# Where the first block's down product keeps its first operand sums, and when the next block's transposing transfers are issued

## The chip, the cores and the metric

The kernel runs on one core of one Trainium2 chip. The metric is device time in microseconds (us) for one execution. A core has five engines that work beside each other and meet at semaphores: TensorE (PE, matrix products), VectorE (DVE), ScalarE (ACT), GpSimd (POOL) and SyncE (SP). SP, ACT and POOL also issue DMA transfers, each from its own queue and in its own order. An engine executes its instructions in the order in which the program lists them, so an instruction that waits holds up everything behind it on that engine.

## The reference, cut to what matters

```python
def reference(A_x, A_wqkv, A_wo, B_x, B_w1, B_w3, B_w2):
    x = A_x                                   # 1 x 2048 x 1024, bf16
    xn = layernorm(x)
    # attention: 32 heads of 32, each position sees 8 positions, 2 apart
    q, k, v = split(xn @ wqkv)                # 1024 x 3072
    o = softmax(q . k[pos - 2*w] * scale) @ v[pos - 2*w]     # w = 0..7
    s = o @ wo                                # 1024 x 1024
    # gated MLP on the same xn
    h = silu(xn @ w1) * (xn @ w3)             # 1024 x 3584 each
    g = silu(h @ w2)                          # 3584 x 1024
    return x + s * g
```

`B_x` is not used. The change touches `h @ w2`, the down product, and the way in which the layer-normed `x` of the next rows reaches the tile from which the next products read it.

## The kernel before, in words

**Rows.** The 2048 rows are worked in two blocks (b = 0, 1) of 1024 rows. A block is two chunks of 512 rows (c = 2b and 2b + 1), a chunk is four steps of 128 rows (`st`, or `g` in the down product). The tile `xT` holds the normed x of the block, transposed: half 0 for the even chunk, half 1 for the odd chunk, in each half 8 row tiles of 512 columns.

**Products.** The large products are written with seven part products instead of eight (2 x 2 blocks, with sums and differences of blocks formed ahead on DVE). For the up products the sums of x stand in the tile `xs` (four parts, fp16). For the down product the blocks are two rows of h (`row` 0 and 1, one for each chunk), two halves of the 3584 inner columns (`fh`) and two halves of the 1024 output columns. The four sums of h are called s1 to s4; s2, s3 and s4 overwrite h in place, s1 has a place of its own. The sums of w2 (called t) were formed in the first block and written to `t_dram`.

**The down product `mlp_down`** of block 0 has seven products in this order. I number them P1 to P7: P1 and P2 (h row 0 with w2), P3 (s2 with T2), P4 (s1 with T1), P5 (s3 with w2), P6 (s4 with T3) and P7 (h row 1 with T4). Each is 4 steps g of 14 matmuls (128 x 128 times 128 x 512), and each streams two operand loads of 896 KB, first and second half. The sums s1, s3 and s2 are written on DVE between P1 and P3. After P4 of a step g, ACT copies the bank (`dsp`), and only then may P5 add to the same bank.

**Buffers for loads.** The operand loads, the x rows of the next chunks, and the weights of what follows share six buffers named `r8`. `Plan.place` (L68) gives each new tile, in the order in which the code lists the work, the buffer whose last user comes earliest in that list. In block 0's down product this gives, with letters for the six buffers:

| tile | first half | second half |
|---|---|---|
| P1 | A | B |
| x of chunk 2, x of chunk 3 | C | D |
| P2 | E | F |
| P3 | A | B |
| P4 | E | F |
| P5 | A | B |
| P6 | E | F |
| P7 | A | B |
| `wo` (two loads), behind P7 | C | E |

**The next block's x.** While block 0's down product runs, the x rows of chunks 2 and 3 are loaded, and ACT takes each chunk's mean and variance (`ln_act`, L430 and L433), the root (L436), and normalises the four steps (L443). DVE adds two tiny instructions for each chunk (L439, L440). Then `ln_td` (L469) issues one transposing transfer for each step from ACT's queue: eight in all, into `xT`. The code lists them with P6 (chunk 2) and P7 (chunk 3).

**Where s1 stands.** `s1v` (L909) puts s1 of steps 0 and 1 into half 0 of `xT` and of steps 2 and 3 into half 1: in each half all but the last of the eight row tiles, 128 of each 256 columns for each step. The cells that follow reads and writes (`s1_cells`, L367) make a transposing transfer wait until P4 has read the s1 that lies under it.

**Order.** Nothing is issued in the order of the code. `Plan` builds the dependences, gives each instruction a due time, and then runs a list schedule: an engine that becomes free takes, of the instructions that are ready, the one with the earliest due time. PE keeps the order of the code. The due time of any other instruction is the earliest due time of those that need it, less its own duration (`limits`, L127). A transfer that fills a buffer is one of those that need the buffer's last users. The durations are constants in the code: 1.3 us of ACT for a transposing transfer, among others. The schedule is made when the program is built; on the chip each engine keeps the order that came out.

Of the kernel before, what the change touches and what calls it, by code (L numbers as in the profile page):

```python
# [224 lines left out]
def kernel(  # L225
# [12 lines left out]
    P = 128  # L238
    S, D, F = 2048, 1024, 3584
    Dh, W, DIL = 32, 8, 2  # L240
    KT = D // P
# [3 lines left out]
    NB = S // BL  # L245
    NST = CH // P
    FT = F // P
    FH = FT // 2
# [4 lines left out]
    NQ = 7  # L253
# [73 lines left out]
    def mm(ps, lhs, rhs, first, rd, last=True, mark=(), st=None):  # L327

        n = len(lhs)
        cut = (lambda a: a) if st is None else (lambda a: a[:, st * P:(st + 1) * P])  # L330

        def emit():
            for k in range(n):
                nc.tensor.matmul(  # L334
                    cut(ps.ap()), lhsT=lhs[k](), rhs=cut(rhs[k]()), start=(first and k == 0),
                    stop=(last and k == n - 1), skip_group_check=not (first and last) or st is not None,
                )
# [16 lines left out]
    def dma(eng, name, o, a, rd, wr, kb, run=1024, late=0.0):  # L354
        e = {SP: nc.sync, POOL: nc.gpsimd, ACT: nc.scalar}[eng]
        occ = {SP: 0.45, POOL: 0.58, ACT: 0.55}[eng]
        plan.op(eng, name, lambda: e.dma_start(out=o(), in_=a()), rd, wr, occ, 0.0, nbytes=kb * 1024, late=late, run=run)
# [5 lines left out]
    def xt_cells(half, kh, st=None):  # L363
        return [("xT", half, (kh * KH + k) * 2 + q // 2, q % 2) for k in range(KH)
                for q in (range(4) if st is None else [st])]

    def s1_cells(g):  # L367
        return [("xT", g // 2, f, g % 2) for f in range(FH)]

    def xs_cells(i):  # L370
        return [("xs", i, k) for k in range(KH)]
# [7 lines left out]
    def r8v(s, dt=BF16):  # L379
        a = s.ap()  # L380
        return a.bitcast(dt) if dt != BF16 else a
# [20 lines left out]
    def xrow(xt, st):  # L402
        return xt.ap().rearrange("p (s d) -> p s d", s=NST)[:, st, :]
# [65 lines left out]
    def ln_td(c, st, xt):  # L469

        half = c % 2
        plan.op(ACT, f"td{c}_{st}", lambda: nc.scalar.dma_start_transpose(  # L472
            out=xT[:, half, :, st * P:(st + 1) * P], in_=xrow(xt, st)),
            [(xt, st)], xt_cells(half, 0, st) + xt_cells(half, 1, st), 1.3, 0.0, nbytes=256 * 1024, run=256)
# [272 lines left out]
    def flush():  # L747
        while pend:
            pend.pop(0)()
# [131 lines left out]
    def mlp_down(b):  # L881
        G = range(NST)
        R = [range(0, FH), range(FH, FT)]
        F_ = [slice(0, FH), slice(FH, FT)]
        gs = [[slice(rr * CH + g * P, rr * CH + (g + 1) * P) for g in G] for rr in range(2)]
# [23 lines left out]
        s1v = lambda g: xT16[:, g // 2].rearrange("p k n -> p (k n)")[:, 0:FH * 256].rearrange(  # L909
            "p (f n) -> p f n", f=FH)[:, :, (g % 2) * P:(g % 2 + 1) * P]  # L910
# [4 lines left out]
        NS = FH * P  # L915
        rhs = rhs_load("w", 0, 0)
        xn = []
        for c in range(2 * b + 2, 2 * b + 4 if b + 1 < NB else 0):
            xt = plan.slot("r8", f"x{c}")
            xn.append(xt)  # L920
            for st in range(NST):
                x_load(c, st, xt)
            ln_act(c, range(NST), xt)
        pa, pb = [], []
        for g in G:
            if g == 2:
                flush()
            pa.append(bank(f"da{b}_{g}"))
            prod(pa[g], g, 0, 0, rhs, True, BF16)
        for g in G:  # L930
            tt("s1", add, lambda g=g: s1v(g), hb(0, 1, g), hb(1, 1, g), hcl(0, 1, g) + hcl(1, 1, g), s1_cells(g), NS, True)
            tt("s3", sub, hf(0, 1, g), hb(0, 0, g), hb(0, 1, g), hcl(0, 0, g) + hcl(0, 1, g), hcl(0, 1, g), NS, True)
        for g in G:
            pb.append(bank(f"db{b}_{g}"))
            cp("dfork", pb[g].ap, pa[g].ap, [pa[g]], [pb[g]])
            tt("s2", sub, hf(0, 0, g), lambda g=g: s1v(g), hb(0, 0, g), s1_cells(g) + hcl(0, 0, g), hcl(0, 0, g), NS, True)
        rhs = rhs_load("w", 1, 0)
        for g in G:
            prod(pa[g], g, 0, 1, rhs, False, BF16)
            gsilu(2 * b, 0, g, pa[g].ap, [pa[g]], 0.48)  # L940
        rhs = rhs_load("t", t=T2)
        su2 = []
        for g in G:
            tt("s4", sub, hf(1, 0, g), hb(1, 0, g), hf(0, 0, g), hcl(1, 0, g) + hcl(0, 0, g), hcl(1, 0, g), NS, True)
        for g in G:
            prod(pb[g], g, 0, 0, rhs, False, FP16)
            su2.append(plan.slot("k2", "dsu"))
            cp("dsu", lambda g=g: f32(su2[g]), pb[g].ap, [pb[g]], [su2[g]])
        rhs = rhs_load("t", t=T1)
        pe, sp5 = [], []  # L950
        for g in G:
            pe.append(bank(f"de{b}_{g}"))
            for q, (wt, ops) in enumerate(rhs):
                mm(pe[g], [lambda g=g, k=k: s1v(g)[:, k, :] for k in range(q * NQ, (q + 1) * NQ)], ops, q == 0,
                   [wt] + s1_cells(g), last=q == 1)
            sp5.append(plan.slot("k2", "dsp"))
            cp("dsp", lambda g=g: f32(sp5[g]), pe[g].ap, [pe[g]], [sp5[g]])
        rhs = rhs_load("w", 1, 1)
        for g in G:
            prod(pe[g], g, 0, 1, rhs, False, FP16)  # L960
            tt("dsb", add, lambda g=g: f32(su2[g]), pe[g].ap, lambda g=g: f32(su2[g]), [pe[g], su2[g]], [su2[g]], 512, False)
            gsilu(2 * b, 1, g, lambda g=g: f32(su2[g]), [su2[g]], 0.54)
        rhs = rhs_load("t", t=T3)
        for g in G:
            if b + 1 < NB:
                ln_td(2 * b + 2, g, xn[0])
            prod(pb[g], g, 1, 0, rhs, False, FP16)
            tt("dsa", add, lambda g=g: f32(sp5[g]), pb[g].ap, lambda g=g: f32(sp5[g]), [pb[g], sp5[g]], [sp5[g]], 512, False)
            gsilu(2 * b + 1, 1, g, lambda g=g: f32(sp5[g]), [sp5[g]], 0.54)
        rhs = rhs_load("t", t=T4)  # L970
        for g in G:
            if b + 1 < NB:
                ln_td(2 * b + 3, g, xn[1])
            prod(pb[g], g, 1, 1, rhs, False, BF16)
            gsilu(2 * b + 1, 0, g, pb[g].ap, [pb[g]], 0.48)

# [242 lines left out]
```

## Time and profile before

| what | value |
|---|---|
| median of the runs shown | 728.86 us (3 runs, 727.54 to 733.38) |
| the profiled execution's own time | 730.64 us |
| span of that execution, first to last instruction | 728.8 us |
| mean granted TensorE clock | 0.994 |
| VectorE busy | 640.3 us (88%) |
| ScalarE busy | 383.2 us (53%) |
| transposing transfers | 8, issued from 297.3 to 318.6 us, 8.8 us from issue to landing (median) |
| P2, P3, P4 begin (TensorE) | 269.81, 281.9, 293.98 us |
| P5 begins | 306.06 us |

Times in the profile count from the first instruction of the span. A row of the timeline gives start, duration, engine (a name with a q is the engine's queue: issuing a transfer, or waiting on a semaphore), the line of the code, the operation, and what it writes and reads; "x2" merges two neighbours, and the bracket at the end gives the idle time of the engine just before and what ended it. In the groups and waits, L334 is the line that emits the matmuls, L343 that of all two-operand DVE instructions, L348 that of ACT copies, L357 that of plain transfers, and L472 that of transposing transfers; so a row is told apart by its tiles. Starts that stand inside a merged row were read from narrower windows of the same timeline (P3's from P2's start and 56 matmuls).

### The profile page before, as it was taken

To read this page: it belongs to the slowest core of one execution; us is meant where nothing else is said; L and a number is where in the kernel's file an instruction comes from. 1 tells how busy PE (TensorE), PEld (TensorE's weight loads), DVE (VectorE), ACT (ScalarE), POOL (GpSimd) and SP (SyncE) were. 2 spreads that over 40 slices of the span, in tenths; PEclk is the share of its full clock that TensorE was granted. 3 is DMA by queue.
4 is the path that set the end of the run, shared out by engine and by line. 5 is a ranking of instruction groups with operands and counts; after the bars stand their busy time and mean duration, and the time that the engine had idled before them with its cause. 6 is when DMAs were issued, how large, how long until landed. Compare 5 with 4: busy or idle time off the path is not lost.

```text
span 728.8 us, 9155 instructions
## 1 busy us (share of the span) xinstructions
PE 714.8 (98%) x3372; PEld 345.6 (47%) x3372; DVE 640.3 (88%) x860; ACT 383.2 (53%) x656; POOL 25.5 (4%) x54
## 2 busy tenths in 40 slices
PE   7999999999999999998999999999999999999997
PEld 5655544444444444443455554444444444444443
DVE  6998999798999999359999899789999967999527
ACT  7754465575656698232444544675565656212233
POOL 0011000100000000000000000000000000000000
PEclk9999999999999999999999999999999999999999
DMA  9869865875546654997355449987555356463522
GB/s 333 303 239 395 278 245 170 274 218 211 179 172 210 224 165 139 208 275 224 115 174 173 169 149 318 295 291 223 188 175 190 115 214 208 152 193 112 173 73 101
DMA packets 127053, 150.54 MB, mean 207 GB/s; under 512 B 12320, under 2 KB 103968, under 8 KB 122656
## 3 DMA queue, kind: packets, MB, share of 16 engines
q1 hardware_dynamic: 113248, 121.65, 51.7%
q0 software_dynamic: 5312, 26.22, 9.5%
q10 hardware_dynamic: 8448, 2.10, 1.9%
q8 instruction: 26, 0.43, 0.3%
q14 instruction: 19, 0.16, 0.1%
HBM read 106.95 MB, written 32.51 MB: 191 GB/s over the span
## 4 chain that ended last, share of the span: by engine, by line
PE 87%; DVE 5%; DMA 4%; ACTq 2%; ACT 1%; issue 0%; SPq 0%; DVEq 0%
PE mm L334 87%; ACTq L472 2%; DVE r L343 2%; DMA r<-in_A_wqkv_dram 2%; DVE h_sb L343 1%; DMA r<-t_dram 1%; DVE xs L343 1%; DMA r<-in_A_x_dram 1%; DVE qo L343 1%; DMA r<-in_B_w_dram 0%; DVE small L411 0%; ACT k L348 0%; PE mm L456 0%; ACT xT L463 0%; DVE r L419 0%
## 5 line engine op out<-in xcount | busy, mean ns | idle before, releaser
L334 PEld LDWEIGHTS <-r 128*128 128x128 f16 (+1 forms) x2288 | 240.6, 107 | 244.5 <-issue 1.5
L334 PE MATMUL mm<-xs,r 128*128 128x512 f16 x1280 | 295.5, 379 | 0.7 <-DVE h_sb L343 0.7
L334 PE MATMUL mm<-xT,r 128*128 128x512 bf16 (+1 forms) x1008 | 228.2, 371 | 0.0
L348 ACT COPY k<-mm 128x512 f32<-128x512 f32 x192 | 111.9, 588 | 94.9 <-PE mm L334 80.2
L334 PE MATMUL mm<-r,h_sb 128*128 128x512 bf16 (+1 forms) x704 | 155.6, 382 | 4.2 <-DMA r<-t_dram 2.5
L343 DVE TENSOR_TENSOR att<-att 128x2048 bf16<-128x2048 bf16 (+4 forms) x132 | 123.7, 952 | 29.5 <-DMA att<-E 20.2
L334 PEld LDWEIGHTS <-h_sb 128*128 128x128 f16 (+1 forms) x800 | 78.7, 98 | 100.2 <-issue 7.1
L348 ACT COPY mm<-mm 128x512 f32<-128x512 f32 x88 | 49.8, 572 | 75.4 <-PE mm L334 49.1
L343 DVE TENSOR_TENSOR att<-qo,kT 128x2048 bf16<-128x2048 bf16 x64 | 77.2, 1216 | 1.6 <-ACT kT L348 1.6
L343 DVE TENSOR_TENSOR att<-E,vT 128x2048 bf16<-128x2048 bf16 x56 | 65.9, 1218 | 0.0
L351 ACT ACTIVATE k<-k 128x512 bf16<-128x512 f32 x56 | 34.8, 631 | 54.8 <-DVE k L343 54.8
L343 DVE TENSOR_TENSOR h_sb<-mm,k 128x512 bf16<-128x512 f32 x96 | 62.2, 682 | 0.4 <-PE mm L334 0.2
L343 DVE TENSOR_TENSOR k<-mm,k 128x512 f32<-128x512 f32 x72 | 47.8, 682 | 13.8 <-PE mm L334 13.7
L343 DVE TENSOR_TENSOR r<-r,r 128x1024 f16<-128x1024 bf16 (+4 forms) x66 | 52.1, 797 | 5.2 <-DMA r<-in_A_wqkv_dram 5.1
L343 DVE TENSOR_TENSOR h_sb<-h_sb,k 128x1024 bf16<-128x1024 bf16 x56 | 36.9, 685 | 12.0 <-ACT k L348 12.0
L351 ACT ACTIVATE h_sb<-mm 128x512 bf16<-128x512 f32 x60 | 35.6, 598 | 20.6 <-PE mm L334 20.3
L343 DVE TENSOR_TENSOR qo<-qo,att 128x2048 bf16<-128x2048 bf16 x32 | 38.9, 1217 | 0.0
L348 ACT CAST k<-mm 128x512 bf16<-128x512 f32 x56 | 32.6, 588 | 10.6 <-PE mm L334 10.3
L343 DVE TENSOR_TENSOR h_sb<-h_sb 128x512 f16<-128x512 bf16 (+1 forms) x72 | 36.6, 570 | 0.0
L343 DVE TENSOR_TENSOR r<-r 128x1024 f16<-128x1024 bf16 (+1 forms) x34 | 25.7, 777 | 0.0
L334 PE MATMUL mm<-r,xT 128*128 128x512 f16 x112 | 24.5, 379 | 0.0
L334 PE MATMUL mm<-h_sb 128*128 128x512 f16 x96 | 22.0, 379 | 0.0
(74 smaller groups left out, 336.9 us busy)
## 6 DMA issues: line engine op xcount, KB each, us to landing
r<-in_B_w_dram SPq DMA_DIRECT2D x42, 512.0 KB, 4.1
s_dram<-r POOLq DMA_DIRECT2D x14, 1024.0 KB, 5.4
r<-t_dram SPq DMA_DIRECT2D x16, 896.0 KB, 6.4
r<-s_dram SPq DMA_DIRECT2D x14, 1024.0 KB, 4.9
r<-in_A_wqkv_dram SPq DMA_DIRECT2D x12, 1024.0 KB, 6.9
r<-in_B_w_dram SPq DMA_DIRECT2D x12, 896.0 KB, 5.4
h_sb<-in_B_w_dram SPq DMA_DIRECT2D x14, 512.0 KB, 9.8
t_dram<-h_sb POOLq DMA_DIRECT2D x14, 512.0 KB, 5.9
```

The costliest lines, as they stand in the source:

```text
L334: nc.tensor.matmul(cut(ps.ap()), lhsT=lhs[k](), rhs=cut(rhs[k]()), start=(first and k == 0), stop=(last and k == n - 1), skip_group_check= ...
L343: plan.op(DVE, name, lambda: fn(out=o(), in0=a(), in1=b()), rd, wr, occ, 0.08, late=late)
L348: plan.op(ACT, name, lambda: nc.scalar.copy(out=o(), in_=a()), rd, wr, occ, 0.11)
L351: plan.op(ACT, name, lambda: nc.scalar.activation(out=o(), in_=a(), func=ACTF.Silu), rd, wr, occ, 0.11, table="silu")
L472: plan.op(ACT, f"td{c}_{st}", lambda: nc.scalar.dma_start_transpose(out=xT[:, half, :, st * P:(st + 1) * P], in_=xrow(xt, st)), [(xt, st)] ...
```

## The change: what it does

For block 0 alone (`b` is 0), s1 moves. Steps 0, 1 and 2 go to the first three of the four parts of `xs`, 14 x 128 columns each. Step 3 goes to half 1 of `xT`, columns 256 to 511 of its first seven row tiles; its sums and what reads them are written with one more dimension (`fold`). Block 1 keeps the old places; there are no transposing transfers in it.

The calls of `ln_td` move up in the code: those of chunk 2 from P6 to P2; those of chunk 3 from P7 to between P3's loads and P3 (steps 0 and 1) and to between P5's loads and P5 (steps 2 and 3).

```diff
-    def s1_cells(g):
-        return [("xT", g // 2, f, g % 2) for f in range(FH)]
+    def s1_cells(b, g):
+        if b:
+            return [("xT", g // 2, f, g % 2) for f in range(FH)]
+        return xs_cells(g) if g < 3 else [("xT", 1, 2 * k + 1, t) for k in range(KT) for t in range(2)]
...
+        fold = lambda a, g: a if b or g < 3 else a.rearrange("p (k h) n -> p k h n", h=2)
...
+        def s1v(g):
+            if b:
+                return xT16[:, g // 2].rearrange("p k n -> p (k n)")[:, 0:FH * 256].rearrange(
+                    "p (f n) -> p f n", f=FH)[:, :, (g % 2) * P:(g % 2 + 1) * P]
+            if g < 3:
+                return xs[:, g].rearrange("p k n -> p (k n)")[:, 0:NS].rearrange("p (f n) -> p f n", f=FH)
+            return xT16[:, 1, 0:NQ, 256:512].rearrange("p k (h n) -> p k h n", h=2)
+
+        def s1t(g, k):
+            return s1v(g)[:, k, :] if b or g < 3 else xT16[:, 1, k // 2, 256 + k % 2 * P:256 + (k % 2 + 1) * P]
...
         rhs = rhs_load("w", 1, 0)
         for g in G:
+            if xn:
+                ln_td(2 * b + 2, g, xn[0])
             prod(pa[g], g, 0, 1, rhs, False, BF16)
             gsilu(2 * b, 0, g, pa[g].ap, [pa[g]], 0.48)
         rhs = rhs_load("t", t=T2)
+        for st in (0, 1) if xn else ():
+            ln_td(2 * b + 3, st, xn[1])
...
         rhs = rhs_load("w", 1, 1)
+        for st in (2, 3) if xn else ():
+            ln_td(2 * b + 3, st, xn[1])
...
         rhs = rhs_load("t", t=T3)
         for g in G:
-            if b + 1 < NB:
-                ln_td(2 * b + 2, g, xn[0])
             prod(pb[g], g, 1, 0, rhs, False, FP16)
...
         rhs = rhs_load("t", t=T4)
         for g in G:
-            if b + 1 < NB:
-                ln_td(2 * b + 3, g, xn[1])
             prod(pb[g], g, 1, 1, rhs, False, BF16)
```

More of the change, by code (lines that the diff above doesn't have):

```diff
@@ L884, in mlp_down @@
         F_ = [slice(0, FH), slice(FH, FT)]
+        NS = FH * P
+        fold = lambda a, g: a if b or g < 3 else a.rearrange("p (k h) n -> p k h n", h=2)
         gs = [[slice(rr * CH + g * P, rr * CH + (g + 1) * P) for g in G] for rr in range(2)]
@@ L907, in prod @@
                    [wt] + h_cells(fs, row, [g]), last=q == 1)
-        s1v = lambda g: xT16[:, g // 2].rearrange("p k n -> p (k n)")[:, 0:FH * 256].rearrange(
-            "p (f n) -> p f n", f=FH)[:, :, (g % 2) * P:(g % 2 + 1) * P]
+        def s1v(g):
[7 more added lines that the diff above has]
+            return s1v(g)[:, k, :] if b or g < 3 else xT16[:, 1, k // 2, 256 + k % 2 * P:256 + (k % 2 + 1) * P]
         hb = lambda fh, row, g: (lambda: h_sb[:, F_[fh], gs[row][g]])
@@ L914, in mlp_down @@
         hcl = lambda fh, row, g: h_cells(R[fh], row, [g])
-        NS = FH * P
         rhs = rhs_load("w", 0, 0)
@@ L930, in mlp_down @@
         for g in G:
-            tt("s1", add, lambda g=g: s1v(g), hb(0, 1, g), hb(1, 1, g), hcl(0, 1, g) + hcl(1, 1, g), s1_cells(g), NS, True)
+            tt("s1", add, lambda g=g: s1v(g), lambda g=g: fold(hb(0, 1, g)(), g), lambda g=g: fold(hb(1, 1, g)(), g), hcl(0, 1, g) + hcl(1, 1, g), s1_cells(b, g), NS, True)
             tt("s3", sub, hf(0, 1, g), hb(0, 0, g), hb(0, 1, g), hcl(0, 0, g) + hcl(0, 1, g), hcl(0, 1, g), NS, True)
@@ L935, in mlp_down @@
             cp("dfork", pb[g].ap, pa[g].ap, [pa[g]], [pb[g]])
-            tt("s2", sub, hf(0, 0, g), lambda g=g: s1v(g), hb(0, 0, g), s1_cells(g) + hcl(0, 0, g), hcl(0, 0, g), NS, True)
+            tt("s2", sub, lambda g=g: fold(hf(0, 0, g)(), g), lambda g=g: s1v(g), lambda g=g: fold(hb(0, 0, g)(), g), s1_cells(b, g) + hcl(0, 0, g), hcl(0, 0, g), NS, True)
         rhs = rhs_load("w", 1, 0)
         for g in G:
+            if xn:
+                ln_td(2 * b + 2, g, xn[0])
             prod(pa[g], g, 0, 1, rhs, False, BF16)
@@ L953, in mlp_down @@
             for q, (wt, ops) in enumerate(rhs):
-                mm(pe[g], [lambda g=g, k=k: s1v(g)[:, k, :] for k in range(q * NQ, (q + 1) * NQ)], ops, q == 0,
-                   [wt] + s1_cells(g), last=q == 1)
+                mm(pe[g], [lambda g=g, k=k: s1t(g, k) for k in range(q * NQ, (q + 1) * NQ)], ops, q == 0,
+                   [wt] + s1_cells(b, g), last=q == 1)
             sp5.append(plan.slot("k2", "dsp"))
```

## The prediction, made before the changed kernel was run

> **What bounds the kernel.** I read the page's first part, then what TensorE waited for, then the timeline of block 0's down product.
>
> ```profile
> PE 714.8 (98%) x3372; PEld 345.6 (47%) x3372; DVE 640.3 (88%) x860; ACT 383.2 (53%) x656; POOL 25.5 (4%) x54
> ...
> PE mm L334 <- DMA r<-t_dram: 2.5, 1, 2.5
> ...
> PE mm L334 <- ACT k L348: 1.7, 1, 1.7
> ```
>
> TensorE is the bound: 14.0 us idle in 728.8, some 9.8 of it ahead of the first products and behind the last. Inside the run two waits stand out, 2.5 and 1.7 us, both in this down product. No change here can win more than these two and what hangs on them.
>
> ```profile
> 297.26 6.23 ACTq L472 DMA_TRANSPOSE xT<-r  x2
> 303.53 0.59 ACT L348 COPY k<-mm 128x512 f32<-128x512 f32 x1 [5.75 <-PE mm L334]
> 303.56 5.51 ACTq L472 DMA_TRANSPOSE xT<-r  x2
> ...
> 309.19 7.12 ACTq L472 DMA_TRANSPOSE xT<-r  x2
> ...
> 316.35 0.59 ACT L348 COPY k<-mm 128x512 f32<-128x512 f32 x1 [6.65 <-issue]
> 316.37 4.65 ACTq L472 DMA_TRANSPOSE xT<-r  x2
> 316.99 16.78 PE L334 MATMUL mm<-r,h_sb 128*128 128x512 bf16 x77 [1.69 <-ACT k L348]
> ...
> 327.78 1.22 SPq L357 DMA_DIRECT2D E<-att  x2
> ...
> 329.10 0.54 SPq L357 DMA_DIRECT2D r<-t_dram  x1
> ...
> 336.30 12.42 PE L334 MATMUL mm<-r,h_sb 128*128 128x512 f16 x49 [2.54 <-DMA r<-t_dram]
> ```
>
> This is the timeline from P4's end on. Eight transposing transfers hold ACT's queue for 23.5 us (6.23 + 5.51 + 7.12 + 4.65), and the `dsp` copies stand between them. The fourth copy, ready when P4 ends (306.2), runs at 316.35; P5's last step waits for it: the 1.69 us. The exponential of the next attention also stands behind the transfers (321.19, idle 4.25 before it), so its results leave for `E` only at 327.78. P7's second load stands behind these on SP's queue: its buffer is free when P5 ends (about 320), it is issued at 329.10, lands at 336.26, and TensorE waits 2.54 us.
>
> ```profile
> 327.00:333.00 6.00, 6.00 (x30) 2.70 (x29) 6.00 (x8) 1.56 (x4) 1.11 (x2) 1.00 0.65 176
> 333.00:339.00 6.00, 3.46 (x13) 1.34 (x12) 5.61 (x7) 2.14 (x4) 0.00 (x0) 0.86 1.08 359
> 339.00:345.00 6.00, 6.00 (x25) 2.57 (x24) 6.00 (x8) 0.74 (x2) 0.00 (x0) 0.86 0.40 146
> ```
>
> The windows (the figure behind POOL is the granted clock) show a price behind that second wait: the clock falls to 0.86 over 12 us, half of it slow. P7's last 49 matmuls go from 336.30 to 348.56, where the next product begins: 12.26 us against 49 x 0.2158 = 10.57 at the pace of P2 to P4 (56 in 12.085). That is 1.69 us more. The first wait left the clock at 1.00. So what can go is 1.69 + 2.54 + 1.69 = **5.92 us**. A rule speaks against the third term: the Trainium skill, "TensorE: Matmul & The Clock Gate", section "What's actually happening", has the clock drop after at least one idle window of about 3.4 us. By it a gap of 2.54 us would leave the clock alone and the sum would be 4.23 us; the row of 0.86 decides against it.
>
> **The change part by part.** *s1's new place.* The four sums keep their count; a sum takes 1.083 us. Matmuls with `xs` and with `xT` both take 379 ns: nothing there. The folded sums of step 3 are not in the trace: at half rate they would cost 2 x 1.08 us of DVE, at best nothing; I take nothing, since they keep the row's element counts. P3's step 3 needs the second of them at 291 us, DVE wrote it by 278.3. Either end is hidden by 12 us.
>
> *The transposing transfers no longer wait for P4* (but for the last two). Still eight, from the same queue. What lets them start is the normalising, now at 283.64 to 294.2, since nothing needed it early. So the move alone would gain about 2 us of start.
>
> *The buffers turn over differently*, and this decides. With chunk 2's last user listed in P2, buffer C is free for P4. By the rule of `place`: P3 keeps A, B; P4 gets **C** and E; P5 F, A; P6 B, C; P7 E and **D** (chunk 3's); `wo` F, A. So P4's first load must wait until all four transfers of chunk 2 have landed, and P7's second load for those of chunk 3. The due times follow: P4's load is due before P4, so chunk 2's transfers, normalising, root and variances get due times ahead of all of chunk 3's work and of P2's activations, where they had been the last of all.
>
> I place them by hand, with the trace's durations. Chunk 2's statistics start at 250.18 as now; a mean with its read-out takes 1.05 us, a variance 1.13, four pairs 8.7; eight copies and activations due earlier come between (about 4.0): 262.9. Root with its table load 1.6, two `uc` copies 1.0: 265.5. The two tiny DVE instructions each stand behind one of about 1.1: 266.6. Four normalisings 4 x 1.14, two `dfork` copies 1.0, and the rest of a started chunk 3 statistic: the transfers start at about **273**, before P4 by 21 us. The two `uc` copies come about 1.5 us later than now, and so does the first sum; P3 needs s2 at 281.9 and has it at 271.2 now: hidden by 9 us.
>
> How long do four transfers take? Contended, in the rows above, from the first issue (297.3) to the fourth landing, which released the load of `wo` into C (315.44): 18.1 us. Alone:
>
> ```profile
> q10 hardware_dynamic: 1719, 0.42, 100.4%
> ...
> 276.00:278.00 2.00, 2.00 (x11) 0.88 (x9) 2.00 (x3) 1.98 (x5) 0.00 (x0) 1.00 0.00 0
> 278.00:280.00 2.00, 2.00 (x11) 0.93 (x10) 2.00 (x3) 1.97 (x3) 0.00 (x0) 1.00 0.00 0
> ```
>
> The first row is the transposing queue from 308 to 310 us: 1719 packets in 2 us. A transfer is 1056 of them (8448 over eight), so 1.23 us. The windows show that now no DMA runs from 276 to 280. P3's loads end at 276; then four transfers take 4.9 us of DMA; with the tail of a landing I put the last at **284** (bounds 280 and 291.1, the latter by the contended 18.1). P4's first load then takes 6.3 us (median of the four T2 and T1 loads): **290.3**, bounds 286 and 297.4. P4 starts at 293.98. I take no wait, as that stretch lies nearer to the idle row than to the contended one. Of the rate, the Trainium skill, "Advanced Engine Details and Errata", section "X-Bar Transpose (TRN2)", says that a transposing DMA is as fast as a regular one. The page's queues disagree: 2.10 MB in 1.9% of 728.8 us is 152 GB/s, against 121.65 MB in 51.7%, 323 GB/s. By that rule the four would take 3.2 us instead of 4.9, with the same sum.
>
> *What now stands behind them.* On ACT: P2's four activations and chunk 3's statistics, some 3 us later than planned. The first activation frees the bank for P4 at 294; it would end by 284. Chunk 3's normalising ends at about 299 to 302; two transfers of 2.5 to 3.5 us each stand before the first and second `dsp` copy, which P5 needs at 306.2 and 309.3; I get 302.5 and 307. The third and fourth follow at once, and the last two transfers come behind the fourth copy: the **1.69 us** go. On SP: P4's first load holds P5's first, needed 12 us later. P7's second load waits for the last transfer, issued by 313.5 and landed by about 322 (8.8 us); with 7.2 us to land it is there at 329, needed at 332. The attention's `E` transfers now stand behind it, not ahead: **2.54 and 1.69 us** go. POOL's queue gets nothing new.
>
> **Sum.** 730.64 for the profiled execution less 5.92 is 724.7. That execution was 1.78 us above the median, so by the median 728.86 - 5.92 = 722.9; I forecast **723 us**. Behind P7 everything moves up together: TensorE ran without a gap for 383.67 us there. DVE can follow: it idled 11.4 and 7.8 us waiting for `att` and the exponential, both of which come earlier.
>
> **Rivals.** *Forecast (0.60):* both waits go, P4 is in time: 721 to 725.5. *P4 waits a little (0.18):* the transfers take the contended 18.1 us even there; P4's load lands at 297.4, 3.4 us late for its first matmul, with up to 1.7 of slow clock: 5.1 of 5.92 are given back, 728.0; range 725 to 729. For it: P3's loads run to 276. Against it: the idle DMA behind them. *The waits only move (0.10):* chunk 3's two transfers before the second `dsp` copy take 4 us each, as the longest did (4.14): P5 waits again, up to 1.7, and P7's load another 2 to 3: 726 to 729. *Slower (0.12):* the planner doesn't bring chunk 2's normalising forward, and it ends at 288.8, as now. Then the fourth landing is at 288.8 + 18.1 = 306.9, P4's load at 313.2: 19.2 us of wait, 1.7 of slow clock, less 5.9: 743.9. It decides from where P4's load lands after 293.98 + 5.92 - 1.69 = 298.2; if half came forward, 735. For it: P2's activations and chunk 3's work share ACT, which is full from 250 to 283. Against it: the due times.
>
> **Numbers.** Eight in ten: from 720.5 (the forecast less the spread of the runs, about 0.3%) to 730, which takes in the second and third cases and leaves out the slower one. A measurement of this kernel can tell about 1% from no change, 7.3 us; the largest gain that I can name is 5.92. Faster by over 1%: 0.14, if run spread adds to the full gain; within 1%: 0.75; slower: 0.11.
>
> **What would show it.** Transposing transfers from about 273, not 297; the normalising of chunk 2 ahead of the activations into `xs`; no TensorE wait on ACT's copies at P5; none on `t_dram` at P7 and a clock of 1.00 there; the first P4 load issued 3 to 4 us later than 280.57 and landed by 294. The prediction is wrong if a gap opens at 294 with the `t_dram` load behind `xT<-r` on SP's queue, or if a gap appears in block 1, where I expect none.

## The result and the profile after

| | before | after |
|---|---|---|
| median (six runs each, taken together) | 730.7 us (727.54 to 733.38) | 724.6 us (723.91 to 725.93) |
| ratio, 95% interval | | 0.9914 (0.9889 to 0.9938) |
| the profiled execution's own time | 730.64 us | 724.38 us |
| its span | 728.8 us | 722.6 us |
| mean granted clock | 0.994 | 0.996 |

The changed kernel is 6.1 us faster by the medians and 6.26 us by the profiled executions; 5.92 were forecast. It ends inside the forecast's own range, 721 to 725.5. The 723 us of the forecast counted from 728.86, the median of the three runs of before known then; from the 730.7 of all six the same 5.92 give 724.8. The lines of the changed file stand two further down than before: the transposing transfers are L474, normalising L445; the matmuls (L334), two-operand DVE instructions (L343) and ACT copies (L348) keep theirs.

The first part of the page of after, and the whole list of what TensorE waited for (us in total, times, longest):

```profile
PE 710.1 (98%) x3317; PEld 345.0 (48%) x3372; DVE 640.2 (89%) x860; ACT 383.6 (53%) x656; POOL 25.5 (4%) x54
```

```profile
PE mm L458 <- DVE r L421: 2.2, 2, 1.2
PE mm L319 <- DVE k L317: 1.2, 1, 1.2
PE mm L334 <- DVE h_sb L343: 0.7, 1, 0.7
```

The two waits of block 0's down product, on ACT's copy and on the load from `t_dram`, are gone, and no new one stands in their place: what is left was there before. The busy time of PE is not to be compared with the 714.8 of before, since 55 matmul records are missing in this trace (3317 of 3372). The starts tell more. TensorE's timeline of after, from P4 on:

```profile
293.86 9.23 PE L334 MATMUL mm<-r,xs 128*128 128x512 f16 x42
302.92 3.19 PE L334 MATMUL mm<-r,xT 128*128 128x512 f16 x14
305.94 36.42 PE L334 MATMUL mm<-r,h_sb 128*128 128x512 bf16 x166
342.20 1.89 PE L334 MATMUL mm<-r,qo 128*128 128x512 bf16 x7
```

P4 reads its sums from `xs` for three steps and from `xT` for one. P5 to P7 are one row without a bracket: from 305.94 to the next product at 342.20 are 36.26 us, and 168 matmuls at the pace of P2 to P4 are 168 x 0.2158 = 36.25. Before, the same stretch took 348.56 - 306.06 = 42.50. The windows of after, over the same times in which the clock was 0.86 before (the figure ahead of the last two is the granted clock):

```profile
327.00:333.00 6.00, 6.00 (x30) 2.70 (x28) 4.84 (x7) 1.83 (x3) 1.11 (x2) 1.00 1.08 358
333.00:339.00 6.00, 6.00 (x30) 2.68 (x29) 6.00 (x9) 1.71 (x3) 0.00 (x0) 1.00 0.51 185
339.00:345.00 6.00, 5.95 (x28) 2.71 (x28) 6.00 (x6) 2.34 (x5) 0.00 (x0) 1.00 0.47 152
```

ACT's timeline of after shows what let the waits go:

```profile
270.02 1.35 ACTq L474 DMA_TRANSPOSE xT<-r  x1
271.41 4.53 ACTq L474 DMA_TRANSPOSE xT<-r  x1
276.04 3.27 ACTq L474 DMA_TRANSPOSE xT<-r  x2
...
293.74 1.25 ACTq L474 DMA_TRANSPOSE xT<-r  x1
...
297.14 1.41 ACTq L474 DMA_TRANSPOSE xT<-r  x1
...
306.14 0.58 ACT L348 COPY k<-mm 128x512 f32<-128x512 f32 x1 [2.44 <-PE mm L334]
306.20 8.00 ACTq L474 DMA_TRANSPOSE xT<-r  x2
...
317.48 1.06 ACT L693 ACTIVATE att<-att 128x1024 f32<-128x1024 f32 x1
```

Four transfers go out from 270 on. The fourth `dsp` copy runs at 306.14, as soon as P4's last step ends. As before, six transfers stand ahead of it; but the last of these is out by 298.55, where before they held the queue from 297.26 to 316.31. The two behind it hold ACT's queue for 8.00 us when no copy is due any more. SP's queue of after:

```profile
280.45 1.27 SPq L357 DMA_DIRECT2D r<-t_dram  x2
281.96 10.95 SPq L357 DMA_DIRECT2D r<-in_B_w_dram  x2
...
304.63 15.80 SPq L357 DMA_DIRECT2D r<-t_dram  x3
320.48 1.54 SPq L357 DMA_DIRECT2D r<-in_A_wo_dram  x2
328.38 1.22 SPq L357 DMA_DIRECT2D E<-att  x2
```

P4's two loads are issued at 280.45 and 281.37. P7's second load is the last of the row at 304.63; it is out by 320.4 (before: 329.10), ahead of the `E` transfers (328.38). Both loads of `wo` follow at once.

### The profile page after: what moved, and what is told of

The parts are those of the page before. It is cut to its first block, busy times and chain, and to the rows that moved or that the text cites. A ratio compares the mean times of both kernels' runs of the same rounds, so it can differ in the third digit from the quotient of the medians.

```text
span 722.6 us, 9090 instructions
## 1 busy us (share of the span) xinstructions
PE 710.1 (98%) x3317; PEld 345.0 (48%) x3372; DVE 640.2 (89%) x860; ACT 383.6 (53%) x656; POOL 25.5 (4%) x54
## 4 chain that ended last, share of the span: by engine, by line
PE 90%; DMA 4%; DVE 4%; issue 1%; ACT 0%; SPq 0%; DVEq 0%
PE mm L334 90%; DMA r<-in_A_wqkv_dram 2%; DVE r L343 2%; DVE h_sb L343 1%; DMA t_dram<-h_sb 1%; DMA h_sb<-in_B_w_dram 1%; DMA r<-in_A_x_dram 1%; DMA r<-in_B_w_dram 0%; DVE qo L343 0%; DVE small L413 0%; PE mm L458 0%; ACT xT L465 0%; DVE r L421 0%; SPq L357 0%; ACT qo L348 0%
## 5 line engine op out<-in xcount | busy, mean ns | idle before, releaser
L334 PEld LDWEIGHTS <-r 128*128 128x128 f16 (+1 forms) x2288 | 240.8, 107 | 244.8 <-issue 1.7
L334 PE MATMUL mm<-xs,r 128*128 128x512 f16 x1280 | 295.6, 379 | 0.8 <-DVE h_sb L343 0.7
L334 PE MATMUL mm<-xT,r 128*128 128x512 bf16 (+1 forms) x968 | 225.6, 371 | 2.1
L348 ACT COPY k<-mm 128x512 f32<-128x512 f32 x192 | 111.9, 587 | 81.9 <-PE mm L334 78.1
L334 PE MATMUL mm<-r,h_sb 128*128 128x512 bf16 (+1 forms) x693 | 152.8, 379 | 0.6
L343 DVE TENSOR_TENSOR att<-att 128x2048 bf16<-128x2048 bf16 (+4 forms) x132 | 123.5, 950 | 21.4 <-DMA att<-E 20.1
L334 PEld LDWEIGHTS <-h_sb 128*128 128x128 f16 (+1 forms) x800 | 78.3, 98 | 94.4
L348 ACT COPY mm<-mm 128x512 f32<-128x512 f32 x88 | 49.8, 572 | 82.9 <-PE mm L334 49.8
L343 DVE TENSOR_TENSOR att<-qo,kT 128x2048 bf16<-128x2048 bf16 x64 | 77.1, 1215 | 0.0
L343 DVE TENSOR_TENSOR att<-E,vT 128x2048 bf16<-128x2048 bf16 x56 | 65.8, 1216 | 0.0
L343 DVE TENSOR_TENSOR h_sb<-mm,k 128x512 bf16<-128x512 f32 x96 | 62.4, 681 | 0.4 <-PE mm L334 0.2
L343 DVE TENSOR_TENSOR k<-mm,k 128x512 f32<-128x512 f32 x72 | 47.7, 682 | 14.4 <-PE mm L334 14.4
L343 DVE TENSOR_TENSOR r<-r,r 128x1024 f16<-128x1024 bf16 (+4 forms) x66 | 52.2, 796 | 3.5 <-DMA r<-in_A_wqkv_dram 3.3
L343 DVE TENSOR_TENSOR h_sb<-h_sb,k 128x1024 bf16<-128x1024 bf16 x56 | 36.9, 684 | 12.9 <-ACT k L348 12.8
L351 ACT ACTIVATE h_sb<-mm 128x512 bf16<-128x512 f32 x60 | 35.6, 597 | 18.2 <-PE mm L334 18.1
L343 DVE TENSOR_TENSOR qo<-qo,att 128x2048 bf16<-128x2048 bf16 x32 | 38.9, 1216 | 0.0
L348 ACT CAST k<-mm 128x512 bf16<-128x512 f32 x56 | 32.5, 585 | 10.7 <-PE mm L334 10.5
L343 DVE TENSOR_TENSOR h_sb<-h_sb 128x512 f16<-128x512 bf16 (+1 forms) x72 | 36.5, 570 | 0.0
L343 DVE TENSOR_TENSOR r<-r 128x1024 f16<-128x1024 bf16 (+1 forms) x34 | 25.7, 777 | 0.0
L334 PE MATMUL mm<-h_sb 128*128 128x512 f16 x96 | 22.0, 379 | 0.0
L343 DVE TENSOR_TENSOR r<-r,xs 128x1024 bf16<-128x1024 bf16 (+1 forms) x13 | 7.2, 565 | 13.3 <-ACT r L348 12.4
```

Of the source, the lines that this page charges most:

```text
L334: nc.tensor.matmul(cut(ps.ap()), lhsT=lhs[k](), rhs=cut(rhs[k]()), start=(first and k == 0), stop=(last and k == n - 1), skip_group_check= ...
L348: plan.op(ACT, name, lambda: nc.scalar.copy(out=o(), in_=a()), rd, wr, occ, 0.11)
L351: plan.op(ACT, name, lambda: nc.scalar.activation(out=o(), in_=a(), func=ACTF.Silu), rd, wr, occ, 0.11, table="silu")
```

## Experiments

The theory of the prediction is *queue positions*: the fourth copy stands behind transfers on ACT, P7's load behind `E` on SP, and where both are freed, 5.92 us go. A first rival is *in series*: behind those two waits stands a chain of other work of nearly the same length, so that freeing only the queues gains little. A second question is what each half of the change does: the new place of s1, and the earlier listing of the transfers, which moves due times and buffers. "Stretch" below is the time from P4's first matmul to the first product behind P7: 54.58 us before, 48.34 after. All ratios are against the kernel before on the same chip.

### The place alone

s1 moved as in the change; the calls of `ln_td` stay with P6 and P7, as before.

```diff
         for g in G:
-            if xn:
-                ln_td(2 * b + 2, g, xn[0])
             prod(pa[g], g, 0, 1, rhs, False, BF16)
...
         rhs = rhs_load("t", t=T3)
         for g in G:
+            if xn:
+                ln_td(2 * b + 2, g, xn[0])
             prod(pb[g], g, 1, 0, rhs, False, FP16)
...
         for g in G:
+            if xn:
+                ln_td(2 * b + 3, g, xn[1])
             prod(pb[g], g, 1, 1, rhs, False, BF16)
```

> The changed kernel with s1 in its new place, but the transposing transfers listed with P6 and P7 again, as before. So the buffers turn over as before (P4's first load goes to E, not to chunk 2's C) and chunk 2's work keeps its late due times. Theory 'place': what held the queue of ScalarE at P5 was that the transfers could not start until P4 had read s1. Then six of the eight start at about 289 us instead of 297, the fourth copy behind P4 runs at about 311 instead of 316, before P5 needs it, P7's second load leaves ahead of the attention's E transfers, no wait is left at P5 or P7, and the time is that of the changed kernel: about 6 us under the kernel before. Theory 'listing' (the prediction's: the buffers and due times decide, the move alone gains about 2 us of start): the transfers start some 2 us earlier, the copies still come late to P5 by up to 1.7 us, P7's wait stays near 2.5 us, and the time is within 0 to 2 us of the kernel before.

Measured: 729.2 us, ratio 0.9973 (0.9955 to 0.9991). TensorE's timeline of this kernel:

```profile
306.29 36.42 PE L334 MATMUL mm<-r,h_sb 128*128 128x512 bf16 x168
...
352.91 1.89 PE L334 MATMUL mm<-xT,r 128*128 128x512 bf16 x8
356.90 2.60 PE L334 MATMUL mm<-xs,r 128*128 128x512 f16 x8 [2.10 <-DVE r L343]
359.29 2.94 PE L334 MATMUL mm<-h_sb,qo 128*128 128x512 f16 x8
```

The theory of the place is right about the waits and that of the listing about the time. The transfers start at 288.37 instead of 297.26, and both waits are gone in full: the stretch is 342.55 - 294.21 = 48.34 us, as in the change. But the next block then waits 2.10 us for a sum of weights that DVE forms (`r<-r,r`), and 16 matmuls take 5.17 us (356.90 to 362.07) instead of 3.45. DVE's rows in the three kernels, first before, then this kernel, then after:

```profile
340.85 1.22 DVE L343 TENSOR_TENSOR h_sb<-r,r 128x2048 f16<-128x2048 bf16 x1
...
356.09 1.23 DVE L343 TENSOR_TENSOR r<-r,r 128x2048 f16<-128x2048 bf16 x1 [0.93 <-DMA r<-in_A_wqkv_dram]
```

```profile
334.98 1.23 DVE L343 TENSOR_TENSOR qo<-E,vT 128x2048 bf16<-128x2048 bf16 x1 [4.37 <-DMA E<-att]
...
341.40 1.22 DVE L343 TENSOR_TENSOR h_sb<-r,r 128x2048 f16<-128x2048 bf16 x1
...
355.63 1.22 DVE L343 TENSOR_TENSOR r<-r,r 128x2048 f16<-128x2048 bf16 x1
```

```profile
331.24 1.23 DVE L343 TENSOR_TENSOR h_sb<-r,r 128x2048 f16<-128x2048 bf16 x1 [1.12 <-DMA r<-in_A_wo_dram]
...
338.79 1.22 DVE L343 TENSOR_TENSOR qo<-E,vT 128x2048 bf16<-128x2048 bf16 x1
...
351.88 1.21 DVE L343 TENSOR_TENSOR r<-r,r 128x2048 f16<-128x2048 bf16 x1
```

The sum ends at 357.32, 356.85 and 353.09; TensorE could use it at 360.65, 354.64 (for this kernel: 352.91 and eight matmuls at pace) and 354.29. Before, DVE was 3.3 us ahead. With s1 moved alone, TensorE is 6.0 us earlier and DVE only 0.5: 2.2 us late. In the change DVE is 4.2 us earlier: on time by 1.2 us.

The rows also say where DVE gains them. Up to the sums of x (`xs<-xT`) the two kernels are level: 320.11 in the change, 320.62 here. Then DVE stands 4.37 us until `E` lands here, but 1.12 us in the change, where it forms the sums of `wo` (`h_sb<-r,r`) in that time. It can, as both loads of `wo` are out by 322; here the second takes the buffer of P6 and is issued at 330.21. (A run further below asks whether that load is needed.)

### Is it DVE's backlog?

The place alone again, and before, each without 24 of DVE's instructions, about 27 us: offsets 2 to 7 of the products with v are left out in chunk 1's attention.

```diff
-            for w0 in (2, 4, 6):
+            for w0 in (2, 4, 6) if c != 1 else ():
```

> The kernel with s1 alone moved, and with work left out: of the second attention's products with v only offsets 0 and 1 are formed and added, offsets 2 to 7 are left out (24 VectorE instructions of about 1.14 us, 27 us, in chunk 1 alone). Theory 'backlog': with s1 alone moved TensorE gains 6.2 us in the down product and waits 2.1 us at the first product with summed weights (and runs slowly behind it), since VectorE, which had idled on the last transposing transfers and on E, comes to these sums with attention work still ahead of them. With that work left out the sums are done in time, the wait and the slow clock go, and the time falls to that of the changed kernel, 6 us under the kernel before. Rival: the sums wait for the load of the weights; then the wait stays and the time stays near 729.

> The kernel before with the same VectorE work left out: control for the run with s1 alone moved. Theory 'backlog': its lost time lies at P5 and P7, ahead of that work, so it stays within 1.5 us of the kernel before (730.5). If it falls by 3 us or more, the missing work is worth something by itself in block 1 and only the difference of the two runs counts.

Measured: 725.15 us, ratio 0.9931 (0.9916 to 0.9946), for the place with less work; 730.51, ratio 1.0002 (0.9986 to 1.0018), for before with less work. Of the first, TensorE's row of the same product, and DVE's sum:

```profile
355.33 1.89 PE L334 MATMUL mm<-xs,r 128*128 128x512 f16 x8
```

```profile
350.58 1.22 DVE L343 TENSOR_TENSOR r<-r,r 128x2048 f16<-128x2048 bf16 x1
```

The bracket is gone; the sum ends at 351.80, 3.5 us ahead. (TensorE has another wait in this kernel, 1.05 us for an ACT copy at 346.70.) So 27 us of DVE are worth nothing to the kernel before, and some 3 us once s1 is moved (0.9973 to 0.9931). That the place alone gains so little is DVE's backlog, shown by taking it away.

The trace of before with less work shows something else. P4 starts 2.00 us later there (295.98), yet the first product behind P7 comes at 348.71, only 0.15 us later than before: P5's wait, which I had expected to stay, is not there, and P7's is the same 2.54 us. So there the end of the stretch hangs on something other than TensorE's own start.

### The queue positions alone

Three edits of before, without the change: all of `E`'s transfers of chunk 1 from POOL's queue, so that P7's load no longer stands behind any; the fourth `dsp` copy on DVE, so that it no longer stands behind ACT's transfers; and both.

```diff
-    dma((POOL, SP)[sq % 2], f"E{c}",
+    dma((POOL, POOL if c == 1 else SP)[sq % 2], f"E{c}",
```

```diff
-            cp("dsp", lambda g=g: f32(sp5[g]), pe[g].ap, [pe[g]], [sp5[g]])
+            if b == 0 and g == 3:
+                plan.op(DVE, "dsp", lambda g=g: nc.vector.tensor_copy(out=f32(sp5[g]), in_=pe[g].ap()),
+                        [pe[g]], [sp5[g]], 0.6, 0.08)
+            else:
+                cp("dsp", lambda g=g: f32(sp5[g]), pe[g].ap, [pe[g]], [sp5[g]])
```

> The kernel before, with one edit: all four E transfers of the second attention (chunk 1) are issued from GpSimd, none from SyncE. Theory 'queue': P7's second load was late because it stood behind E on SyncE's queue. Then it is issued at about 320 us, when P5 has freed its buffer, lands by 328.5, ahead of 333.8, and P7's wait (2.54 us, and 0.16 of a matmul's drain that the idle time doesn't count) and the slow clock behind it (1.69 us) go: 4.4 us less; P5's wait of 1.69 us stays. Rival 'bandwidth': the load is late because the DMA engines are full of transposing packets; then it lands at 334 or later although it leaves at 320, and less than 1 us is gained.

> The kernel before, with one edit: the fourth copy behind P4 in the first block runs on VectorE, the other three stay on ScalarE. Both theories: P5's wait of 1.69 us goes. Theory 'in series': P7's second load leaves SyncE when E does, and E hangs on the exponential, which stands behind all eight transposing transfers on ScalarE; taking one copy of 0.6 us out of that queue brings it forward by no more than about 0.6 us. So P7's wait grows from 2.5 to about 3.8 us, the slow clock stays, and the time falls by 0 to 1 us only. Theory 'terms add' (as the prediction's sum has it): P7's wait stays 2.5 us and the time falls by 1.7 to 1.9 us.

> The kernel before with both edits: E of the second attention from GpSimd, and the fourth copy on VectorE. s1 and the transposing transfers stay where they were. Theory 'queues': the whole gain of the change is the two queue positions; both waits and the slow clock go, 6.2 us less than the kernel before, the same time as the changed kernel. Rival: the early start of the transposing transfers is worth something beyond (less contention later, an earlier attention); then this version stays 1 us or more above the changed kernel.

| edit of before | median us | ratio (95%) | stretch us |
|---|---|---|---|
| `E` from POOL | 730.79 | 1.0000 (0.9972 to 1.0028) | 53.45 |
| copy on DVE | 730.78 | 0.9993 (0.9973 to 1.0013) | 53.89 |
| both | 732.81 | 1.0010 (0.9981 to 1.0039) | 50.70 |

Each edit does what it says: P7's second load goes out by 319.9 with `E` on POOL; P5's wait is gone with the copy on DVE. Neither gains, and at P7 each meets a wait that none of the theories had. TensorE's row there, first with `E` from POOL, then with the copy on DVE:

```profile
334.44 13.93 PE L334 MATMUL mm<-r,h_sb 128*128 128x512 f16 x56 [2.85 <-DVE k L343]
```

```profile
334.89 2.00 PE L334 MATMUL mm<-r,h_sb 128*128 128x512 f16 x7 [2.92 <-DVE k L343]
```

With `E` from POOL the load, issued at 319.54, takes 12.6 us and is there at 332.1, in time; now P7 waits for DVE's additions (`k`), which come late since DVE stands 10.03 us for the exponential (9.07 with the copy on DVE). TensorE's timeline with both edits:

```profile
331.95 9.22 PE L334 MATMUL mm<-r,h_sb 128*128 128x512 f16 x42 [0.99 <-DVE k L343]
342.22 3.18 PE L334 MATMUL mm<-r,h_sb 128*128 128x512 f16 x14 [1.05 <-DVE k L343]
...
361.12 2.91 PE L334 MATMUL mm<-xs,r 128*128 128x512 f16 x8 [3.64 <-DVE r L343]
```

Both old waits are gone and the stretch is 3.9 us shorter (0.6 us of this is a later start of P4). But DVE still stands 9.20 us for the exponential, which is behind the transfers on ACT, and then 4.98 for `E`; so its additions come late for P7, and its sums for the next block come 3.64 us late. *In series* holds: the two waits that TensorE shows in before cover a third path through DVE of almost their length. Freeing the queues is not enough; DVE has to be brought forward too.

### The slower rival: transfers that come late

The change with chunk 2's transfers given a due time 36 us and 26 us later.

```diff
-def ln_td(c, st, xt):
+def ln_td(c, st, xt, late=0.0):
...
-   ... 1.3, 0.0, nbytes=256 * 1024, run=256)
+   ... 1.3, 0.0, nbytes=256 * 1024, run=256, late=late)
...
-                ln_td(2 * b + 2, g, xn[0])
+                ln_td(2 * b + 2, g, xn[0], 36.0)
```

> The changed kernel, with the due times of chunk 2's four transposing transfers set 36 us later; nothing else. The buffers stay as in the change, so P4's first load still waits for these transfers. On ScalarE they come behind P2's activations, at about 284 us instead of 270. Theory (the prediction's slower rival): the four take 11.3 us from first issue to last landing, as in the changed kernel, so the load is issued at about 296 and lands at 302 to 305; P4 starts 9 to 11 us late, the clock is slow for up to 1.7 us more, and the time is about 734 to 736 us, above the kernel before. Rival 'there is slack elsewhere': P4's late start is made good later; then less than half of that is seen.

> As the run with 36 us, but 26 us later: chunk 2's transfers come between P2's activations, from about 277 us instead of 270. Theory: last landing at about 289, P4's first load issued then and landed at 295 to 297, so TensorE waits 1 to 3 us at P4 and the clock may fall behind it: 724 to 727 us, between the changed kernel and the kernel before. If the load lands before 293.9 there is no wait and the time is the changed kernel's: then the margin of the change is more than 7 us of transfer start.

Measured: 741.17 us, ratio 1.0141 (1.0119 to 1.0164), with 36; 724.8, ratio 0.9921 (0.9905 to 0.9938), with 26. TensorE's timeline with 36, then its weight load at the start of P4 with 26:

```profile
307.77 10.58 PE L334 MATMUL mm<-r,xs 128*128 128x512 f16 x42 [12.82 <-DMA r<-t_dram]
```

```profile
294.43 1.62 PEld L334 LDWEIGHTS <-xs 128*128 128x128 f16 x9 [0.54 <-DMA r<-t_dram]
```

This is the rival that makes the change slower, in the place that was named: P4's load needs the buffer of chunk 2, and waits for its fourth transfer. The time is above the 734 to 736 us that I expected, as I had the load at 6 to 9 us; issued at 295.75 it lands 12.0 us later, at 307.75, beside transposing transfers and the attention's. With 26 the load goes out at 289.46 instead of 281.37, takes 4.9 us and lands at 294.36. P4 begins with it, at 294.43, where the pace of P2 and P3 would have it at 294.21 (264.00 + 140 x 0.2158). So this run stands at the edge: the load's issue has some 8 us to spare in the change, and not more.

### What else brings DVE forward

The change with the second load of `wo` held back until P6 has ended; the place alone, with chunk 3's transfers listed with P6 instead of P7; and before with that listing.

```diff
             prod(pb[g], g, 1, 0, rhs, False, FP16)
+            if b == 0:
+                plan.ops[-1].wr.append(("p6", g))
...
-                lambda dh=dh: wo_r[:, :, dh * CH:(dh + 1) * CH], [], [wot], 1024)
+                lambda dh=dh: wo_r[:, :, dh * CH:(dh + 1) * CH], list(hold) if dh else [], [wot], 1024)
...
-        wots = wo_load()
+        wots = wo_load([] if b else [("p6", 3)])
```

```diff
+            if b + 1 < NB:
+                ln_td(2 * b + 3, g, xn[1])
             prod(pb[g], g, 1, 0, rhs, False, FP16)
...
-            if b + 1 < NB:
-                ln_td(2 * b + 3, g, xn[1])
             prod(pb[g], g, 1, 1, rhs, False, BF16)
```

> The changed kernel, with one edit: in the first block the second load of wo may not be issued before P6 has ended (about 330 us instead of 321), which is when it could be issued with s1 alone moved. New theory 'third wait': in the run with s1 alone moved, TensorE lost no time in the down product, but VectorE did the wo sums late, behind attention instructions that wait for E, since wo's second load had to wait for a buffer of P6; its backlog then made TensorE wait 2.1 us for the sums of the next block's weights, with a slow clock behind it. Then the same shows here: P5 to P7 without a wait, VectorE idle 3 to 5 us on E ahead of the wo sums, TensorE waiting 2 to 3 us at the first product with summed weights (about 355 us), 728 to 730 us. Rival 'late x': that loss came from chunk 3's late transposing transfers (VectorE waited 7.3 us for them); they are early here, so the time stays that of the changed kernel, 724.6.

> The kernel with s1 alone moved, with one edit: chunk 3's transposing transfers are listed with P6 instead of P7 (chunk 2's stay with P6). Then P4's first load does not wait for transfers, chunk 2's work keeps its late due times, but wo's second load gets chunk 3's buffer D instead of P6's E. Theory 'third wait': wo's second load is issued at about 320 us instead of 330, the wo sums come ahead of the attention on VectorE, no wait is left at 355 us, and the time is the changed kernel's, 724 to 726 us: then the early transposing transfers of the change are not needed, only s1's place and the earlier load of wo. Rival: the early transfers themselves are needed; 728 to 730 us as with s1 alone moved.

> The kernel before, with one edit: chunk 3's transposing transfers are listed with P6 instead of P7. s1 stays in xT. wo's second load gets chunk 3's buffer, as above. All theories that need the waits at P5 and P7 gone: both are still there (1.7 and about 2.5 us), so the time is the kernel before's within 1 us. If instead it falls by 3 us or more, the earlier wo load alone was the gain.

*`wo` held:* 725.79 us, ratio 0.9947 (0.9926 to 0.9968): not the 728 to 730 of the theory of the third wait. The change beside the late-transfer runs had 0.9923. The load goes out at 329.13, the sums of `wo` come at 341.13, and DVE stands 3.40 us for `E`, much as with the place alone. Yet `r<-r,r` is on time, at 351.95. For in this run the last transfers landed earlier: DVE has its x at 317.60 instead of 320.11, and `E` leaves at 325.87 instead of 328.38. (The profile of the change's second run, below, has 319.47 and 327.73.) So most of the gain does not need the early `wo`. That the earlier transfers keep DVE on time in its place is read from these rows and not tested, and what carries the change, where both are there, stays open. The two ratios differ by 0.0024, 1.8 us, and their intervals overlap.

*Chunk 3 with P6:* I expected a gain, or at worst the time of the place alone. Measured: 734.58 us, ratio 1.0067 (1.0044 to 1.0089). ACT's timeline, then TensorE's:

```profile
301.96 10.98 ACTq L474 DMA_TRANSPOSE xT<-r  x2
312.99 0.59 ACT L348 COPY k<-mm 128x512 f32<-128x512 f32 x1 [10.52 <-issue]
```

```profile
313.62 6.10 PE L334 MATMUL mm<-r,h_sb 128*128 128x512 bf16 x14 [4.26 <-ACT k L348]
```

Here all transfers run from 294 on, beside the attention's and the products' loads; two of them hold the queue for 10.98 us, a `dsp` copy stands behind them again, and DVE waits 15.23 us for `att`. With before's place the same listing gives 730.7, ratio 1.0005 (0.9981 to 1.0030), and P7's wait stays (3.15 us); P5's, which I expected too, is not in this trace, where P4 starts 1.2 us later than in before. So the place allows early transfers, and the listing decides when they go: from 270 us in the change, 288 with the place alone, 294 here. Where they fall into the contended stretch, P5's wait comes back, and worse. The change's listing has four of them done by 281.4, in a stretch with few loads.

### The change once more

> The changed kernel itself, beside the two with later due times, for a comparison on the same chip: 6 us under the kernel before, no wait inside the run.

Measured: 725.23 us, ratio 0.9923 (0.9901 to 0.9945). TensorE has no gap left in block 0's down product, and none of the kernels run is measurably faster than the change.

## Why the prediction was right, and where it was not

**The sum.** 1.69 + 2.54 + 1.69 = 5.92 us was forecast for the stretch behind P4; it is shorter by 42.50 - 36.26 = 6.24. The missing 0.32 are the two gaps' other part: the profile's idle time counts from the modelled end of the last matmul, 379 ns after its start, while the pace is 216 ns. So each gap hides another 0.16 us, and 5.92 + 2 x 0.16 = 6.24. The third term, the slow clock, was right to be counted: windows of 1.00 stand where 0.86 stood. "Half of it slow" was a wrong reading of those windows: the clock was at half for 3.41 of the 12 us (rows in the last section). Nothing was taken for the folded sums of step 3, and rightly: they take 1.085 us each.

**The transfers.** Placed at 273, behind all four normalisings, they start at 270.02, behind two; the fourth, placed at 284, has landed by 281.37, when SP lets P4's load go. First issue to fourth landing is 11.3 us, against 11 as placed and 18.1 contended: the duration was right, the start 3 us early. P4's load then takes 9.8 us instead of 6.3, P5's being issued 0.6 us behind it, and lands at 291.2, where I had 290.3. That it comes so near is luck in part: 2.6 us too early and 3.5 us too long nearly cancel. It was there 2.7 us ahead of P4, against the 3.7 that I gave it.

**ACT and SP.** The `dsp` copies were put at 302.5 and 307, with the fourth after that; they run at 297.08, 300.10, 303.12 and 306.14, each as soon as its bank is full. The two transfers ahead of them held the queue for 1.25 and 1.41 us, not 2.5 to 3.5 each. P7's second load was put at 322 and goes at 320; here, too, two errors cancel, since the last transfer left at 307.7 instead of 313.5 and took 12.3 us to land instead of 8.8. Both waits go for the reasons given.

**"The move alone would gain about 2 us of start"** is the step that failed. With the place alone the transfers start 8.9 us earlier (288.37 for 297.26), and both waits go in full. That it gains only some 2 us of time in the end (ratio 0.9973) has another reason, DVE's backlog.

**"DVE can follow: both come earlier"** was right in its conclusion by 1.2 us and wrong in its ground. The exponential comes 5.0 us earlier (317.48 for 322.48), but `att` lands 2.4 us later (310.44 for 308.03) and `E` leaves 0.6 us later. DVE follows since it stands idle less behind that: from 297 to 340 us, 15.8 us (12.61 + 2.08 + 1.12) against 19.6 before (11.39 + 7.83 + 0.39) and 20.4 with the place alone. I had written down that `wo` would get buffers F and A, and not read from it that its second load then waits for P5 instead of P6: it is out by 322, for 330.21 with the place alone. The run with `wo` held shows that this alone does not decide it.

**"No change here can win more than these two and what hangs on them"** held, but the terms are not free for the taking one by one: with the waits undone at their queues, without the change, the gain was nothing (ratio 1.0010). The list of waits shows the path that ended last, and a path just behind it is in no row of it.

**The rivals.** Slower was priced at 743.9, from the point where P4's load lands after 298.2. Brought about by later due times, it gave 741.2 with a landing at 307.7: the mechanism stands, with a load that takes 12.0 us instead of 6.3. By my own formula (landing less 293.98, 1.7 of slow clock, less 5.9) 307.7 gives 9.5 us slower; 10.4 were measured. "The waits only move" did not occur in the change; with the place and chunk 3 listed with P6 it did at P5, for 4.26 us instead of up to 1.7 (734.6 us).

## What to carry to other kernels

Before summing the waits of the bound engine, take the next engine along the path and read how far ahead of it it is, at the first place behind the waits where the bound engine needs it: a gain larger than that lead (3.3 us here, for a gain of 6.2) is given back in part unless something brings that engine forward as well. Here letting the long transfers start early, when the memory queues rest, removed the waits on queue positions; taking single instructions out from behind the transfers gained no time. And where a change alters which buffer a load gets, go through every load that moves, the ones that come free earlier included.

## What the runs showed of the hardware that was not expected

**The clock falls after shorter gaps than assumed, for a stretch of 3.41 us or more.** Time above the pace of 0.2158 us per matmul, behind a gap of TensorE:

| gap us | kernel, place | extra us |
|---|---|---|
| 1.69 | before, P5 | 0.00 |
| 1.90 | `E` from POOL, at 362 | 0.13 |
| 2.10 | place alone, at 357 | 1.72 |
| 2.54 | before, P7 | 1.69 |
| 2.85 | `E` from POOL, P7 | 1.69 |
| 3.15 | before with chunk 3 with P6, P7 | 1.69 |
| 3.64 | both queue edits, at 361 | 1.72 |
| 4.26 | place, chunk 3 with P6, P5 | 2.93 |
| 12.82 | due time 36 us later, P4 | 1.36 |

Each is from one profiled execution (5.17 us for 16 matmuls at 357, for example, less 3.45). Three windows of before show where the fourth row's price lies (granted clock 1.00, 0.50, 1.00):

```profile
333.91:337.32 3.41, 1.02 (x5) 0.48 (x5) 3.41 (x4) 0.26 (x1) 0.00 (x0) 1.00 1.09 360
337.32:340.73 3.41, 3.41 (x10) 1.22 (x8) 3.41 (x6) 1.12 (x2) 0.00 (x0) 0.50 1.07 372
340.73:344.14 3.41, 3.41 (x17) 1.57 (x16) 3.41 (x4) 0.60 (x1) 0.00 (x0) 1.00 0.18 61
```

P7's matmuls go on at 336.30 at the full clock, and only 1.0 us later the clock is at half, for 3.41 us. The price is half of the slow time in which TensorE works: 3.41 / 2 = 1.7 in five of the rows. Behind the gap of 4.26 us the clock is at half from 312.74 to 319.56, and work began at 313.62: 2.97. Behind that of 12.82 us it is at half from 300.29 to 310.53, and work began at 307.77: 1.38 (windows with these bounds show 0.50).

So in this kernel a gap of 1.9 us costs little more than itself and one of 2.1 us nearly twice itself; these are single gaps, and whether the length decides between them or the moment at which a gap falls is not shown. The Trainium skill, "TensorE: Matmul & The Clock Gate", section "What's actually happening", has the clock drop to half after at least one idle window of about 3.4 us; the four gaps from 2.10 to 3.15 were enough here. It has it return after about 3.4 us of work; an estimate from that figure, 3.4 us at half pace, is 1.7 us, and the five rows agree.

**A transposing transfer's price depends on what runs beside it.** In the stretch of after where the loads rest, the transposing queue moves 2009 packets in 2 us (277 to 279), 1.05 us for the 1056 packets of a transfer, and two transfers hold ACT's queue for 3.27 us. Beside other loads two of them hold it for 8.00 us in after and 10.98 us with chunk 3 listed with P6.
